# One product of an output stage split once more into seven, with its operand sums on GpSimd

## The chip, the cores and the metric

The kernel runs on one core of a Trainium2 chip. The metric is the device time of one execution in microseconds, the median of several runs.

## The reference

Eight batches of linear attention feed one layer of a feed-forward network. q, k and v are 8 x 8 heads x 576 x 64, all float32.

```python
q_s = softmax(q, over the 64 of a head);  k_s = softmax(k, over the 576 of the sequence)
kv  = einsum('bhsd,bhse->bhde', k_s, v)
x   = einsum('bhsd,bhde->bhse', q_s, kv)        # laid out as 4608 tokens x 512
h   = x @ w_in                                  # 512 x 2048
g   = 0.5 * h * (1 + erf(h / sqrt(2)))          # gelu
out = g @ w_out                                 # 2048 x 512
```

## The kernel before

Everything is worked in bfloat16 with float32 sums in PSUM. The 4608 tokens are worked in nine chunks of 512: chunk c (0 to 7) is the first 512 tokens of batch c, chunk 8 the 64 left over of each batch. The program is written out by hand in the order in which each engine gets its instructions; there is no scheduler, so the order in the code is the order in each engine's queue.

A steady chunk (3 to 7) has an h part and a y part. The h part (`h_waves`) computes h with one level of Strassen-Winograd's scheme (seven products for eight) and the gelus on ScalarE, which write g. The operand sums for the products are made by VectorE: `x_sums` makes t1 to t4 out of xT (the tile quad_t), `s_parts` makes s1 to s4 out of g (tiles s5 and s12; s3 overwrites a quarter of g). The y part (`y_phase`) computes the output in the same scheme. Its seven products have 16 matmuls each (two groups of 128 tokens, eight steps of the contraction, 256 columns). They are issued in the order 1, 5, 6, 2, 7, 3, 4, into the three PSUM banks pa (products 1, 6, 7, 4, accumulated), pb (5, then 3) and pc (2). In the code's names the four quarters of the chunk's output are c11, c12, c21 and c22, in two SBUF tiles y_sb. Between the products VectorE and ScalarE combine the banks into them:

```python
tt(two(pb), two(pa), c22)                # after 6: pb = pa + c22, to which product 3 adds
...
tt(c22, two(pa), c22)                    # after 7
...
mm(3, pb, False)
nc.scalar.copy(out=c12, in_=two(pb))
y_store(c, 0, ysb[0])
after(3)
mm(4, pa, False)
```

`tt` (L430) is the helper behind nearly all of VectorE's tensor operations, so they all have its line. L686 is the matmul of `y_phase`, L739 that of the last chunk (`y_last`, whose last product is made in two halves of 128 columns into banks named yd), L498 that of `h_waves`.

The attention of later batches is spread over the y parts through the table `ins`: after product 5 come the exponentials of k of batch nb = c + 2 and the casts of v on GpSimd (`cast_v_all`, L190), after product 6 the sums of q on VectorE (`q_sums`: one long reduce, L263, and a reciprocal) and the scaling of q on GpSimd (`q_scale_parts`, L278), and the loads of batch nb + 1. After product 3 comes `next_x`: the eight matmuls that make x of chunk c + 1 (L353; in chunk 7, 64 small ones, L358) into four banks, their copies into xT (two on ScalarE, two on VectorE), the DMA transpose of q of batch nb, and, where nb is under 8 (c up to 5), the 72 small matmuls of kv (L225) with their normalization. In chunks 6 and 7 there is no kv, in chunk 7 no `q_sums` either. Product 4 follows on TensorE, then the h part of the next chunk.

`touch_s` is a copy of one element on GpSimd that makes GpSimd wait for VectorE's last operand sum before it goes on, so that its work in the y part runs beside PSUM work of VectorE. The banks of PSUM have roles (bb, ba, x0 to x3, kv0, kv1) which `turn_roles` passes round from chunk to chunk. Chunk 2's h part has an order of its own (`mid` is set there). DMAs are issued on SP's queue, in the last chunk on ScalarE's too.

Of the kernel before, what the change touches and what calls it, by code (L numbers as in the profile page):

```python
# [16 lines left out]
def kernel(  # L17
# [174 lines left out]
    def cast_v_all(b):  # L192
        for hp in range(HP):
            cast_v(b, hp, nc.gpsimd)
# [88 lines left out]
    def norm_q(b, i=0, n=1, eng=None):  # L283

        q_sums(b, i, n)
        q_scale(b, eng or nc.gpsimd, i, n)
# [74 lines left out]
                            start=(bb == 0), stop=True, skip_group_check=True,  # L361
                        )

    def x_all(b, banks):

        if "xT" not in st[b]:
            st[b]["xT"] = attn_sb.tile([128, HP, M], BF16, tag="xT", name="xT", bufs=1)
        for hp, i in enumerate(banks):
            st[b][f"x{hp}"] = bank(i)
        x_mm(b, 0)  # L370
        x_mm(b, 1)
        for hp, eng in ((0, "s"), (1, "v"), (2, "s"), (3, "v")):
            x_evac(b, hp, eng)

    def x_evac(b, hp, eng="v"):
# [19 lines left out]
    def s_parts(c, p0, n, which):  # L395

        g = st[c]["g"]
        a, b = slice(p0, p0 + n), slice(p0 + HK, p0 + HK + n)
        lo, hi = slice(0, HT), slice(HT, M)
        a11, a12, a21, a22 = g[:, a, lo], g[:, b, lo], g[:, a, hi], g[:, b, hi]  # L400
        s1, s2, s4 = s5[:, a], s12[:, a, lo], s12[:, a, hi]
        ops = {
            1: (s1, a21, a22, ALU.add), 2: (s2, s1, a11, ALU.subtract),
            3: (a21, a11, a21, ALU.subtract), 4: (s4, a12, s2, ALU.subtract),
        }
        for i in which:
            tt(*ops[i])
# [21 lines left out]
    def tt(out, in0, in1, op=ALU.add, eng=nc.vector):  # L429
        eng.tensor_tensor(out=out, in0=in0, in1=in1, op=op)  # L430
# [33 lines left out]
    def h_waves(c, mid):  # L464
# [7 lines left out]
        sum_w = {3: 3, 5: 0, 6: 1, 7: 2}  # L472
        lo, hi = slice(0, HT), slice(HT, M)
        bank_of = {
            "A": ("bb", "x0", "x3", "ba"), "B": ("kv0", "kv1", "x1", "x2"), "C": ("x1", "x2", "kv0", "kv1"),
        }
        if mid:
            bank_of.update(B=("kv0", "kv1") * 2, C=("x1", "x2") * 2)
# [127 lines left out]
            mm(4, 2, 3)  # L606
        gelu("B", 2, 3)
        gelu("A", 2, 3)
        s_parts(c, 0, 4, (2, 3, 4) if mid else (3, 4))
        s_parts(c, 4, 4, (1, 2, 3, 4))  # L610
        turn_roles()
        if mid:
            roles.update(ba=roles["x2"], x2=roles["ba"])
# [37 lines left out]
    def y_store(c, half, y_sb):  # L651
        j = 2 * half
        dst = out[c * S:c * S + M, :].rearrange("(p j) n -> p j n", j=J)[:, j:j + 2, :]
        nc.sync.dma_start(out=dst, in_=y_sb)
# [4 lines left out]
    def y_operands(c):  # L659
# [8 lines left out]
        }  # L668
        return act, wgt

    def y_phase(c, ins):

        act, wgt = y_operands(c)
        at = {"ya": 2, "yb": 0, "yc": 3} if c == 1 else {"ya": roles["ba"], "yb": roles["bb"], "yc": roles["x0"]}
        pa, pb, pc = (bank(at[n], n) for n in ("ya", "yb", "yc"))
        ysb = [moe_sb.tile([128, 2, DM], FP32, tag="y_sb", name="y_sb", bufs=2) for i in range(2)]
        c11, c12 = ysb[0][:, :, 0:HN], ysb[0][:, :, HN:DM]
        c21, c22 = ysb[1][:, :, 0:HN], ysb[1][:, :, HN:DM]

        def two(ps):  # L680
            return ps.rearrange("p (j n) -> p j n", j=2)

        def mm(m, ps, first):
            for j in range(2):
                for k in range(HK):
                    nc.tensor.matmul(  # L686
                        ps[:, j * HN:(j + 1) * HN], act[m][:, k, j * 128:(j + 1) * 128],
                        wgt[m][:, k, :], start=(first and k == 0 and j == 0),
                        stop=(k == HK - 1), skip_group_check=True,
                    )  # L690

        def after(i):
            for fn in ins.get(i, []):
                fn()

        mm(1, pa, True)
        (nc.vector.tensor_copy if c == 1 else nc.scalar.copy)(out=c11, in_=two(pa))
        after(1)
        mm(5, pb, True)
        nc.vector.tensor_copy(out=c22, in_=two(pb))  # L700
        after(5)
        mm(6, pa, False)
        tt(two(pb), two(pa), c22)
        after(6)
        mm(2, pc, True)
        tt(c11, c11, two(pc))
        after(2)
        mm(7, pa, False)
        tt(c22, two(pa), c22)
        after(7)  # L710
        mm(3, pb, False)
        nc.scalar.copy(out=c12, in_=two(pb))  # L712
        y_store(c, 0, ysb[0])
        after(3)
        mm(4, pa, False)
        nc.scalar.copy(out=c21, in_=two(pa))
        y_store(c, 1, ysb[1])
        after(4)

    def y_last(c):  # L720

        act, wgt = y_operands(c)
        sets = (("ba", "bb", "x0"), ("x2", "x1", "x3"))
        banks = [[bank(roles[r], n)[:, 0:HN] for r, n in zip(s, ("ya", "yb", "yc"))] for s in sets]
        ysb = [moe_sb.tile([128, 2, DM], FP32, tag="y_sb", name="y_sb", bufs=2) for i in range(2)]
        dst = out.rearrange("(j u s) n -> u s j n", j=J, u=2)

        def store(half, j, c0, engs, us=(0, 1)):
            for u, eng in zip(us, engs):
                eng.dma_start(  # L730
                    out=dst[u, M:S, 2 * half + j, c0:c0 + HN],
                    in_=ysb[half][u * R:(u + 1) * R, j, c0:c0 + HN],
                )

        sp, both = nc.sync, (nc.scalar, nc.sync)

        def mm(j, m, ps, first, n=slice(0, HN)):
            for k in range(HK):
                nc.tensor.matmul(  # L739
                    ps[:, n], act[m][:, k, j * 128:(j + 1) * 128], wgt[m][:, k, n],  # L740
                    start=(first and k == 0), stop=(k == HK - 1), skip_group_check=True,
                )

        for j in range(2):
            mm(j, 1, banks[j][0], True)
            nc.scalar.copy(out=ysb[0][:, j, 0:HN], in_=banks[j][0])
        for j in range(2):
            pa, pb, pc = banks[j]
            c11, c12 = ysb[0][:, j, 0:HN], ysb[0][:, j, HN:DM]
            c21, c22 = ysb[1][:, j, 0:HN], ysb[1][:, j, HN:DM]  # L750
            mm(j, 5, pb, True)
            if j:
                store(0, 0, HN, both, (0,))
                store(1, 0, 0, both, (0,))
            nc.scalar.copy(out=c22, in_=pb)
            mm(j, 6, pa, False)
            tt(pb, pa, c22)
            mm(j, 2, pc, True)
            tt(c11, c11, pc)
            store(0, j, 0, both if j else (sp, sp))  # L760
            mm(j, 7, pa, False)
            tt(c22, pa, c22)
            if j:
                nc.scalar.copy(out=c21, in_=pa)
            store(1, j, HN, both if j else (sp, sp))
            mm(j, 3, pb, False)
            nc.scalar.copy(out=c12, in_=pb)
            if j:
                store(0, j, HN, both)
                for r, n in (("kv0", slice(0, 128)), ("kv1", slice(128, HN))):  # L770
                    ps = bank(roles[r], "yd")
                    mm(j, 4, ps, True, n)
                    tt(c21[:, n], c21[:, n], ps[:, n])
                store(1, j, 0, both)
            else:
                store(0, j, HN, (sp,), (1,))
                mm(j, 4, pa, False)
                nc.scalar.copy(out=c21, in_=pa)
                store(1, j, 0, (sp,), (1,))
# [235 lines left out]
    for m in (3, 2, 4, 1):  # L1015
# [11 lines left out]

    y_phase(1, {
        1: [sums[3], lambda: norm_q(2, 0, 2)],
        6: [lambda: norm_q(2, 1, 2, nc.vector), lambda: cast_v_all(3), lambda: xbar_step(2), lambda: exp_q(3)],  # L1030
        2: [lambda: kv_step(2), lambda: exp_k(3)],
        7: [lambda: q_sums(3)],
        3: [lambda: table(AF.Gelu)],
# [12 lines left out]

        nc.gpsimd.tensor_copy(out=scr[:, 2:3], in_=s12[:, HK - 1, HT:HT + 1])

    def next_x(c, nb):
        x_all(c + 1, [roles[n] for n in ("x0", "x1", "x2", "x3")])  # L1050
        if nb <= B:
            xbar_step(nb)
        if nb < B:
            kv_tiles(nb, (roles["kv0"], roles["kv1"]))
            kv_step(nb, lambda: x_sums(c + 1, (1,)))
            x_sums(c + 1, (2,))
        else:
            x_sums(c + 1, (1, 2))

    for c in range(2, B + 1):  # L1060
        nb = c + 2
        h_waves(c, q_late if c == 2 else None)
        yi = {}
        if nb <= B:
            yi[1] = [lambda: exp_q(nb)]
            yi[6] = [lambda: q_sums(nb), lambda: q_scale_parts(nb)]
            yi[7] = [lambda: table(AF.Gelu)]
        if nb + 1 < B:
            yi[6].append(lambda: load(nb + 1))
        elif nb + 1 == B:  # L1070
            yi[6].append(load_qrest)
        if nb < B:
            yi[5] = [lambda: exp_k(nb), touch_s, lambda: cast_v_all(nb)]
        if c < B:
            yi[3] = [lambda: next_x(c, nb)]
            y_phase(c, yi)
        else:
            y_last(c)
# [30 lines left out]
```

## Time and profile before

| what | value |
|---|---|
| median of 3 runs | 257.45 us (257.31 to 257.54) |
| profiled execution | 257.79 us |
| its span | 255.7 us |
| granted TensorE clock | 0.998 |
| busy: TensorE | 248.6 us, 97% |
| busy: VectorE | 189.8 us, 74% |
| busy: ScalarE | 189.1 us, 74% |
| busy: GpSimd | 53.9 us, 21% |

PE is TensorE, PEld its weight loads, DVE VectorE, ACT ScalarE, POOL GpSimd, SP the queue that issues DMAs. A q behind an engine's name (ACTq) is its sequencer. A group's row gives the line, the engine, the operation with the tiles that it writes and reads, shapes and count, then the busy time, the mean length of one in ns, and the idle time ahead of them. The timeline gives the start, the length and the instructions, with merged equal ones; lengths of merged rows include the overlap of one instruction with the next. Product 1 starts at 85.40 in chunk 2, 111.52 in chunk 3, 137.33 in chunk 4, 163.08 in chunk 5, 188.89 in chunk 6, 214.01 in chunk 7 and 239.23 in chunk 8.

### The profile page before, as it was taken

The numbers are of one execution on the slowest core, as the hardware profiler recorded it, in microseconds if no ns is written. First come the engines' busy times: TensorE is split into PE (matmuls) and PEld (weight loads), VectorE is DVE, ScalarE is ACT, GpSimd is POOL, SyncE is SP. The second block draws the span as 40 slices with busy tenths as digits, with TensorE's granted clock in tenths as the row PEclk, the third lists the DMA queues.
The fourth block names the chain that finished last, engine by engine and source line by source line (L and its number), as shares of the span: only waits on it lengthen the run. The fifth ranks groups of instructions, "written<-read, shape, count | busy, mean of one in ns | idle before, by whom it ended". The sixth has DMA issues, their size and how long they took to land.

```text
span 255.7 us, 6526 instructions
## 1 busy us (share of the span) xinstructions
PE 248.6 (97%) x2678; PEld 195.8 (77%) x2678; DVE 189.8 (74%) x337; ACT 189.1 (74%) x323; POOL 53.9 (21%) x85
## 2 busy tenths in 40 slices
PE   7899999999999999999999999999999999999993
PEld 3444444448888888888888888888888888888883
DVE  1878698877987985898589858985798689448931
ACT  4776878699887986899688968895887687068711
POOL 1530023000705065005500560056000700000000
PEclk9999999999999999999999999999999999999999
DMA  7999999994289997933693369203400240040033
GB/s 239 401 363 424 402 408 398 399 410 178 53 256 380 267 355 234 318 143 102 228 313 142 91 222 245 45 0 118 133 3 0 103 145 3 0 167 3 0 82 86
DMA packets 43166, 50.23 MB, mean 196 GB/s; under 512 B 20224, under 2 KB 30464, under 8 KB 42880
## 3 DMA queue, kind: packets, MB, share of 16 engines
q1 hardware_dynamic: 42416, 49.13, 56.5%
q10 hardware_dynamic: 720, 0.69, 1.1%
q8 instruction: 21, 0.34, 0.5%
q14 instruction: 9, 0.07, 0.1%
HBM read 36.70 MB, written 9.44 MB: 180 GB/s over the span
## 4 chain that ended last, share of the span: by engine, by line
PE 79%; DMA 16%; DVE 1%; issue 1%; ACT 1%; ACTq 0%; SPq 0%
PE ya L686 19%; PE qa L498 19%; PE yb L686 9%; PE qb L498 9%; DMA w<-in_moe_w_in_dram 6%; PE ps L387 6%; DMA f<-in_k_dram 5%; PE qc L498 5%; PE yc L686 5%; DMA f<-in_v_dram 3%; PE ya L739 2%; DMA touch<-in_moe_w_in_dram 2%; PE yb L739 1%; PE kv L225 1%; PE ps L353 1%; DVE s L430 1%
## 5 line engine op out<-in xcount | busy, mean ns | idle before, releaser
L498 PEld LDWEIGHTS <-quad_s 128*128 128x128 bf16 x448 | 43.8, 98 | 5.2
L686 PEld LDWEIGHTS <-g 128*128 128x128 bf16 x448 | 43.2, 98 | 6.0 <-issue 0.4
L686 PEld LDWEIGHTS <-s 128*128 128x128 bf16 x336 | 32.8, 98 | 4.2 <-DVE s L430 0.4
L498 PEld LDWEIGHTS <-wi_bf 128*128 128x128 bf16 x336 | 32.9, 98 | 4.0 <-issue 0.2
L278 POOL TENSOR_TENSOR e<-e,recq 128x256 bf16<-128x256 bf16 x40 | 24.2, 642 | 30.7 <-DVE recq L264 21.1
L498 PE MATMUL qa<-quad_t,quad_s 128*128 128x256 bf16 x224 | 29.2, 273 | 0.0
L430 DVE TENSOR_TENSOR qb<-qa,r 128x512 f32<-128x512 f32 x28 | 18.2, 695 | 14.2 <-PE qa L498 9.6
L387 PE MATMUL ps<-xT,wi_bf 128*128 128x512 bf16 x128 | 28.1, 379 | 0.2 <-ACT xT L380 0.2
L686 PE MATMUL yb<-wo_bf,s 128*128 128x256 bf16 x224 | 26.9, 273 | 0.1
L686 PE MATMUL ya<-w,g 128*128 128x256 bf16 x224 | 26.8, 273 | 0.0
L263 DVE TENSOR_REDUCE qsum<-e 128x16 f32<-128x1024 bf16 (+1 forms) x12 | 20.9, 1740 | 4.6 <-ACT e L173 4.5
L387 PEld LDWEIGHTS <-wi_bf 128*128 128x128 bf16 x128 | 12.4, 98 | 15.3 <-issue 0.7
L393 ACT ACTIVATE g<-ps 128x512 bf16<-128x512 f32 x32 | 17.6, 602 | 6.2 <-PE ps L387 5.8
L173 ACT ACTIVATE e<-f 128x512 bf16<-128x512 f32 (+1 forms) x42 | 20.5, 557 | 2.0 <-DMA f<-in_q_dram 1.9
L522 ACT ACTIVATE g<-r 128x512 bf16<-128x512 f32 x28 | 17.3, 631 | 6.1 <-DVE r L430 6.1
L522 ACT ACTIVATE g<-qc 128x512 bf16<-128x512 f32 x28 | 15.2, 594 | 7.5 <-PE qc L498 7.5
L269 POOL TENSOR_TENSOR e<-e,recq 128x1024 bf16<-128x1024 bf16 (+1 forms) x4 | 9.3, 2330 | 48.5 <-DVE recq L264 41.9
L430 DVE TENSOR_TENSOR r<-qa,r 128x512 f32<-128x512 f32 x28 | 18.0, 683 | 0.9 <-PE qa L498 0.7
L178 ACT ACTIVATE ek<-f 128x2304 bf16<-128x2304 f32 (+1 forms) x10 | 17.2, 1726 | 1.1 <-DMA f<-in_k_dram 1.1
L190 POOL CAST v_aug<-f 128x576 bf16<-128x576 f32 x25 | 17.0, 716 | 3.6 <-DMA f<-in_v_dram 3.5
L378 DVE CAST xT<-ps 128x512 bf16<-128x512 f32 x18 | 11.6, 682 | 8.0 <-PE ps L353 6.4
L712 ACT COPY y_sb<-yb 128x512 f32<-128x512 f32 x7 | 4.1, 585 | 17.2 <-PE yb L686 16.1
(96 smaller groups left out, 442.0 us busy)
## 6 DMA issues: line engine op xcount, KB each, us to landing
out_dram<-y_sb SPq DMA_DIRECT2D x16, 512.0 KB, 3.4
f<-in_k_dram SPq DMA_DIRECT2D x6, 1152.0 KB, 9.6
f<-in_v_dram SPq DMA_DIRECT2D x6, 1152.0 KB, 9.2
f<-in_q_dram SPq DMA_DIRECT2D x6, 1024.0 KB, 7.0
w<-in_moe_w_in_dram SPq DMA_DIRECT2D x6, 512.0 KB, 9.0
f<-in_v_dram SPq DMA_DIRECT2D x8, 288.0 KB, 6.5
f<-in_q_dram SPq DMA_DIRECT2D x4, 512.0 KB, 8.9
w<-in_moe_w_out_dram SPq DMA_DIRECT2D x2, 1024.0 KB, 11.5
```

The source lines that it names most:

```text
L173: nc.scalar.activation(out=dst[:, i], in_=src[:, u], func=AF.Exp)
L178: nc.scalar.activation(out=ek[b % 2][:, i:i + n], in_=st[b]["kf"][:, i:i + n].rearrange("p x (n d) -> p x n d", n=NS), func=AF.Exp,)
L190: eng.tensor_copy(out=o, in_=i)
L263: nc.vector.reduce_sum(out=qsum, in_=st[b]["eq"][:, :, i * w:(i + 1) * w, :], axis=AX.X)
L278: nc.gpsimd.tensor_tensor(out=e, in0=e, op=ALU.mult, in1=st[b]["recq"][:, j, i:i + 4].unsqueeze(2).to_broadcast([128, 4, D]),)
L378: nc.vector.tensor_copy(out=st[b]["xT"][:, hp, :], in_=ps)
L387: nc.tensor.matmul(ps, wi_bf[:, dm, t * 128:(t + 1) * 128], st[c]["xT"][:, dm, :], start=(dm == 0), stop=(dm == NDM - 1),)
L393: nc.scalar.activation(out=st[c]["g"][:, t, :], in_=ps, func=AF.Gelu)
L430: eng.tensor_tensor(out=out, in0=in0, in1=in1, op=op)
L498: nc.tensor.matmul(held[kind, q][:, u], w, mov[m][:, k], start=(m in (1, 5) and u == 0 and k == 0), stop=(k == 1), skip_group_check=True,)
L522: nc.scalar.activation(out=g[:, t:t + 2, half], in_=held[kind, q], func=AF.Gelu)
L686: nc.tensor.matmul(ps[:, j * HN:(j + 1) * HN], act[m][:, k, j * 128:(j + 1) * 128], wgt[m][:, k, :], start=(first and k == 0 and j == 0), ...
```

## The change

In chunks 3 to 7 product 3 (s4 of g by the lower right quarter of w_out) is no longer 16 matmuls of 256 columns into pb but seven second-level products ("sets"), each of four matmuls of 128 columns, 28 in all, each with a weight load of its own as before. Sets 1, 6 and 7 go into a quarter of the bank kv1 (the tile yd, `D`), sets 2, 3, 4 and 5 into the four quarters of the bank of pb (the tile yf, `X`). Set 1 stands behind product 6, sets 6, 5, 2, 4, 3 and 7 behind product 7, where product 3 was. The sums of operands that the sets need are made by GpSimd: four sums of weights once, in chunk 1's y part (`two_begin`, which takes over the buffer of an earlier v), and four sums of s4 in each of the chunks (`sums`, behind `touch_s` after product 5). They are 128 x 512 each.

On VectorE pb = pa + c22 becomes c12 = pa + c22 in SBUF, and five adds bring the sets into c12: a (set 1's u to a quarter), b (u with set 6, to a quarter), c (u with set 7, to two quarters), then, inside `next_x`, e (all of X) and d (one quarter of X again). The add c22 = pa + c22 after product 7 is queued behind c.

Further: one xT copy of `next_x` goes from VectorE to ScalarE in these chunks, and ScalarE's c12 copy falls away; the store of c12 is issued behind `next_x`, so behind the transpose on SP; the first two banks of `h_waves` change places; the casts of v are queued ahead of the h part in chunks 3 to 5; in chunk 2 the sum s1 of rows 4 to 7 is made ahead of s4 of rows 0 to 3; in the last chunk VectorE copies c12 of the second half instead of ScalarE.

```diff
-    def x_all(b, banks):
+    def x_all(b, banks, engs="svsv"):
...
-        for hp, eng in ((0, "s"), (1, "v"), (2, "s"), (3, "v")):
+        for hp, eng in enumerate(engs):
             x_evac(b, hp, eng)
...
-            "A": ("bb", "x0", "x3", "ba"), "B": ("kv0", "kv1", "x1", "x2"), "C": ("x1", "x2", "kv0", "kv1"),
+            "A": ("x0", "bb", "x3", "ba"), "B": ("kv0", "kv1", "x1", "x2"), "C": ("x1", "x2", "kv0", "kv1"),
...
-        s_parts(c, 0, 4, (2, 3, 4) if mid else (3, 4))
-        s_parts(c, 4, 4, (1, 2, 3, 4))
+        if mid:
+            s_parts(c, 0, 4, (2, 3))
+            s_parts(c, 4, 4, (1,))
+            s_parts(c, 0, 4, (4,))
+            s_parts(c, 4, 4, (2, 3, 4))
+        else:
+            s_parts(c, 0, 4, (3, 4))
+            s_parts(c, 4, 4, (1, 2, 3, 4))
...
+    class Two:
...
+        def halves(self, t, ks):
+            return [[t[:, b + 2 * ks.start:2 * ks.stop:2, n:n + 128] for n in (0, 128)] for b in range(2)]
+
+        def weights(self):
+            (b11, b12), (b21, b22) = self.halves(self.raw_w(), slice(0, 4))
+            t1, t2, t3, t4 = (self.w[:, i] for i in range(4))
+            for o, i0, i1 in ((t1, b12, b11), (t2, b22, t1), (t3, b22, b12), (t4, b21, t2)):
+                tt(o, i0, i1, ALU.subtract, eng=nc.gpsimd)
...
+        def sums(self, c):
+
+            (a11, a21), (a12, a22) = self.halves(y_operands(c)[0][self.m], slice(0, 4))
+            s1, s2, s3, s4 = (self.s[:, i] for i in range(4))
+            tt(s1, a21, a22, eng=nc.gpsimd)
+            for o, i0, i1 in ((s2, s1, a11), (s4, a12, s2), (s3, a11, a21)):
+                tt(o, i0, i1, ALU.subtract, eng=nc.gpsimd)
...
+        def mm(self, *sets):
+
+            lo, hi = slice(0, 128), slice(128, 256)
+            A, W, w, s = self.A, self.W, self.w, self.s
+            for m in sets:
+                for i in range(4):
+                    e, o = 2 * i, 2 * i + 1
+                    lhs, rhs, at, r = {
+                        1: (A[:, e, lo], W[:, e, lo], "D", 0),
+                        2: (A[:, o, lo], W[:, o, lo], "X", 0),
+                        3: (s[:, 3, i], W[:, o, hi], "X", 1),
+                        4: (A[:, o, hi], w[:, 3, i], "X", 2),
+                        5: (s[:, 0, i], w[:, 0, i], "X", 3),
+                        6: (s[:, 1, i], w[:, 1, i], "D", 0),
+                        7: (s[:, 2, i], w[:, 2, i], "D", 0),
+                    }[m]
+                    first = at not in self.begun
+                    self.begun.add(at)
+                    nc.tensor.matmul(
+                        getattr(self, at)[:, r * 128:(r + 1) * 128], lhs, rhs,
+                        start=first, stop=(i == 3), skip_group_check=True,
+                    )
+
+        def add(self, what, out):
...
+            X = self.X.rearrange("p (j n m) -> p j n m", j=2, n=2)
+            u = self.D[:, 0:128]
+            o = out.rearrange("p j (n m) -> p j n m", n=2)
+            for i in what:
+                t, x = {
+                    "a": (o[:, 0, 0], u), "b": (o[:, 0, 1], u),
+                    "c": (o[:, 1], u.unsqueeze(1).to_broadcast([128, 2, 128])),
+                    "d": (o[:, 0, 1], X[:, 1, 1]), "e": (o, X),
+                }[i]
+                tt(t, t, x)
...
         mm(6, pa, False)
-        tt(two(pb), two(pa), c22)
+        if t3:
+            tt(c12, halves(pa), c22)
+            t3.begin(c, bank(at["yb"], "yf"), bank(roles["kv1"], "yd"))
+            t3.mm(1)
+            t3.add("a", c12)
+        else:
+            tt(halves(pb), halves(pa), c22)
         after(6)
         mm(2, pc, True)
...
         mm(7, pa, False)
-        tt(c22, two(pa), c22)
+        if t3:
+            t3.mm(6, 5, 2, 4, 3)
+            t3.add("b", c12)
+            t3.mm(7)
+            t3.add("c", c12)
+        tt(c22, halves(pa), c22)
         after(7)
-        mm(3, pb, False)
-        nc.scalar.copy(out=c12, in_=two(pb))
-        y_store(c, 0, ysb[0])
-        after(3)
+        if not t3:
+            mm(3, pb, False)
+            nc.scalar.copy(out=c12, in_=halves(pb))
+            y_store(c, 0, ysb[0])
+            after(3)
+        else:
+            ins[3][0](lambda: t3.add("ed", c12))
+            y_store(c, 0, ysb[0])
         mm(4, pa, False)
...
             mm(j, 3, pb, False)
-            nc.scalar.copy(out=c12, in_=pb)
+            (nc.vector.tensor_copy if j else nc.scalar.copy)(out=c12, in_=pb)
...
-    def next_x(c, nb):
-        x_all(c + 1, [roles[n] for n in ("x0", "x1", "x2", "x3")])
+    def next_x(c, nb, fn=lambda: None):
+        x_all(c + 1, [roles[n] for n in ("x0", "x1", "x2", "x3")], "svsv" if c == 2 else "svss")
         if nb <= B:
             xbar_step(nb)
+
+        def first():
+            x_sums(c + 1, (1,))
+            fn()
+
         if nb < B:
             kv_tiles(nb, (roles["kv0"], roles["kv1"]))
-            kv_step(nb, lambda: x_sums(c + 1, (1,)))
-            x_sums(c + 1, (2,))
-        else:
-            x_sums(c + 1, (1, 2))
+            kv_step(nb, first)
+        else:
+            first()
+        x_sums(c + 1, (2,))
...
     for c in range(2, B + 1):
         nb = c + 2
+        if 2 < c < B - 2:
+            cast_v_all(nb)
...
         if nb < B:
-            yi[5] = [lambda: exp_k(nb), touch_s, lambda: cast_v_all(nb)]
+            yi[5] = [lambda: exp_k(nb), touch_s]
+            if c == 2:
+                yi[5].append(lambda: cast_v_all(nb))
+        if 2 < c < B:
+            yi.setdefault(5, []).append(lambda: two[3].sums(c))
```

More of the change, by code (lines that the diff above doesn't have):

```diff
@@ L669, in y_operands, with __init__, raw_w, begin @@
         return act, wgt
+    class Two:
+        def __init__(self, m, w, s):
+            self.m, self.w, self.s = m, w, s
+        def halves(self, t, ks):
[5 more added lines that the diff above has]
+                tt(o, i0, i1, ALU.subtract, eng=nc.gpsimd)
+        def raw_w(self):
+            return wo_bf[:, DN, HN:DM]
+        def sums(self, c):
[4 more added lines that the diff above has]
+                tt(o, i0, i1, ALU.subtract, eng=nc.gpsimd)
+        def begin(self, c, X, D):
+            self.A, self.W = y_operands(c)[0][self.m], self.raw_w()
+            self.X, self.D = X, D
+            self.begun = set()
+        def mm(self, *sets):
[30 more added lines that the diff above has]
+                tt(t, t, x)
@@ L671, in y_phase, with two_begin @@
+    def two_begin():
+        t = f32in.tile([128, 9, 512], BF16, tag="vf1", name="two", bufs=1)
+        two[3] = Two(3, *(t[:, i:i + 4].rearrange("p x (i n) -> p x i n", i=4) for i in (0, 4)))
+        two[3].weights()
+    two = {}
     def y_phase(c, ins):
@@ L678, in y_phase, with halves @@
         c21, c22 = ysb[1][:, :, 0:HN], ysb[1][:, :, HN:DM]
-        def two(ps):
+        def halves(ps):
             return ps.rearrange("p (j n) -> p j n", j=2)
@@ L694, in after @@
                 fn()
+        t3 = two[3] if c > 2 else None
         mm(1, pa, True)
-        (nc.vector.tensor_copy if c == 1 else nc.scalar.copy)(out=c11, in_=two(pa))
+        (nc.vector.tensor_copy if c == 1 else nc.scalar.copy)(out=c11, in_=halves(pa))
         after(1)
         mm(5, pb, True)
-        nc.vector.tensor_copy(out=c22, in_=two(pb))
+        nc.vector.tensor_copy(out=c22, in_=halves(pb))
         after(5)
         mm(6, pa, False)
-        tt(two(pb), two(pa), c22)
+        if t3:
[5 more added lines that the diff above has]
+            tt(halves(pb), halves(pa), c22)
         after(6)
         mm(2, pc, True)
-        tt(c11, c11, two(pc))
+        tt(c11, c11, halves(pc))
         after(2)
         mm(7, pa, False)
-        tt(c22, two(pa), c22)
-        after(7)
-        mm(3, pb, False)
-        nc.scalar.copy(out=c12, in_=two(pb))
-        y_store(c, 0, ysb[0])
-        after(3)
+        if t3:
[4 more added lines that the diff above has]
+        tt(c22, halves(pa), c22)
+        after(7)
+        if not t3:
[6 more added lines that the diff above has]
+            y_store(c, 0, ysb[0])
         mm(4, pa, False)
-        nc.scalar.copy(out=c21, in_=two(pa))
+        nc.scalar.copy(out=c21, in_=halves(pa))
         y_store(c, 1, ysb[1])
@@ L1029 @@
         1: [sums[3], lambda: norm_q(2, 0, 2)],
-        6: [lambda: norm_q(2, 1, 2, nc.vector), lambda: cast_v_all(3), lambda: xbar_step(2), lambda: exp_q(3)],
+        6: [lambda: norm_q(2, 1, 2, nc.vector), lambda: cast_v_all(3), two_begin, lambda: xbar_step(2), lambda: exp_q(3)],
         2: [lambda: kv_step(2), lambda: exp_k(3)],
@@ L1072 @@
         if nb < B:
-            yi[5] = [lambda: exp_k(nb), touch_s, lambda: cast_v_all(nb)]
+            yi[5] = [lambda: exp_k(nb), touch_s]
[3 more added lines that the diff above has]
+            yi.setdefault(5, []).append(lambda: two[3].sums(c))
         if c < B:
-            yi[3] = [lambda: next_x(c, nb)]
+            yi[3] = [lambda *fn: next_x(c, nb, *fn)]
             y_phase(c, yi)
```

## The prediction

> **What bounds the kernel now.** I read the page's busy shares first, then the chain of waits, then TensorE and VectorE beside each other in the timeline of one steady chunk, and last the groups by form for prices.
>
> ```profile
> PE 248.6 (97%) x2678; PEld 195.8 (77%) x2678; DVE 189.8 (74%) x337; ACT 189.1 (74%) x323; POOL 53.9 (21%) x85
> PE 79%; DMA 16%; DVE 1%; issue 1%; ACT 1%; ACTq 0%; SPq 0%
> ```
>
> TensorE is the bound: busy 97% of the span, and apart from the loads at the start the chain that ends last is TensorE nearly throughout. A matmul taken away is worth its time, and a wait put into TensorE's queue costs its whole length. The chain shows TensorE waiting for VectorE in chunk 2, and in chunk 6 product 3, the next x and product 4 back to back:
>
> ```profile
> 86.55 1.29 DVE s L430 x2
> 87.84 0.05 issue
> 87.89 1.48 PE yb L686 x12
> ...
> 197.79 1.75 PE yb L686 x16
> 199.54 0.56 PE ps L353 x8
> 200.09 1.85 PE ya L686 x16
> ```
>
> In chunk 2, product 5 stops after four of its 16 matmuls until the sum s1 of rows 4 to 7 is written. The timeline of chunk 4, TensorE and then VectorE, from the end of product 3 on (product 1 starts at 137.33):
>
> ```profile
> 147.90 0.63 PE L353 MATMUL ps<-qT,kvc 64*64 64x512 bf16 x8
> 148.36 0.81 PE L225 MATMUL kv<-v_aug,ek 64*64 64x65 bf16 x72
> 149.10 1.92 PE L686 MATMUL ya<-w,g 128*128 128x256 bf16 x16
> ...
> 143.44 2.28 DVE L263 TENSOR_REDUCE qsum<-e 128x32 f32<-128x2048 bf16 x1
> 145.75 0.35 DVE L264 RECIPROCAL recq<-qsum 128x32 f32<-128x32 f32 x1
> 146.02 0.63 DVE L430 TENSOR_TENSOR y_sb<-y_sb,yc 128x512 f32<-128x512 f32 x1
> 146.56 0.68 DVE L430 TENSOR_TENSOR y_sb<-ya,y_sb 128x512 f32<-128x512 f32 x1
> 148.39 1.29 DVE L378 CAST xT<-ps 128x512 bf16<-128x512 f32 x2 [1.15 <-PE ps L353]
> ```
>
> Product 4 accumulates into the bank that the c22 add (146.56) reads. That add ends at 147.24, 1.86 us before product 4 starts at 149.10; VectorE then idles 1.15 us. This slack is what the change spends.
>
> **The change, part by part.** All times below count from the start of product 1 of a chunk.
>
> *Fewer matmul columns.* The prices:
>
> ```profile
> L686 PE MATMUL yb<-wo_bf,s 128*128 128x256 bf16 x224 | 26.9, 273 | 0.1
> L739 PE MATMUL yd<-w,g 128*128 128x128 bf16 x16 | 1.1, 219 | 0.0
> L430 DVE TENSOR_TENSOR y_sb<-ya,y_sb 128x256 f32<-128x256 f32 x2 | 0.8, 424 | 0.9 <-PE ya L739 0.9
> L430 DVE TENSOR_TENSOR y_sb<-y_sb,yd 128x128 f32<-128x128 f32 x2 | 0.6, 286 | 1.1 <-PE yd L739 1.0
> ```
>
> Means are latencies of overlapping matmuls, so I take spacings. Products of 16 start 1.747 us apart (139.08 to 140.82 and so on), 109.2 ns a matmul. The 16 matmuls of yd are the very form that the change uses, one weight load each: 1.06 us from first start to last end, less the last one's 219 ns, over 15 gaps is 56 ns. Product 3 goes from 16 x 109.2 = 1.747 to 28 x 56 = 1.563 us: -0.185 us a chunk, -0.92 over chunks 3 to 7.
>
> The Trainium skill speaks against this step: "TensorE: Matmul & The Clock Gate", section "Back-to-back issue gap", gives about 81 ns for a 128-column matmul in a stream of weight loads and matmuls, and calls the 56 ns an isolated figure. By that, an estimate from the page, product 3 would take 2.27 us and lose 0.52 a chunk; the yd row is such a stream and shows 56, and the measurement decides here.
>
> *The second-level adds on VectorE.* One 512-wide add into PSUM becomes one into SBUF (0.70, same), and adds a (0.29), b (0.29), c (0.42), e (0.65) and d (0.29) come in; ScalarE loses the c12 copy and takes one of VectorE's two xT copies (0.6 each). Where they stand in the queue decides. Set 1 stands behind product 6, so sets 6, 5, 2, 4, 3 start at 5 x 1.747 + 0.22 = 8.96, and set 7, which writes the bank that b reads, at 8.96 + 20 x 0.0558 = 10.08.
>
> - b: VectorE's reduce starts after add a, about 6.4; reduce, reciprocal and the c11 add (2.28, 0.35, 0.63, starts overlapping by 0.09) bring b to 9.6 to 9.9. Set 7 goes at 10.08: 0.15 to spare.
> - c: set 7's last matmul ends at 10.46. Handing on takes 0.055 each way (yd's last end 251.64 to the add's start 251.70; in chunk 2 s1's end 87.83 to product 5 at 87.89). c runs 10.52 to 10.94.
> - kv: half its matmuls write the bank that c reads. Before they start at 148.36 - 137.33 = 11.03, now 0.185 earlier, 10.85, and must wait to 10.99. Bounds: 0.08 to 0.17 for c between 0.36 and 0.45; I take 0.135. That leaves -0.05 in each of chunks 3 to 5: **-0.15**.
> - c22 is now queued behind c: 10.85 to 11.53, and product 4 may start at 11.59. In chunks 3 to 5 TensorE arrives at 11.77 - 0.05 = 11.72, so kv covers it by 0.13. In chunk 6 there is no kv: product 4 began at 200.03 - 188.89 = 11.14, now 11.59: **+0.45** net of the saving. In chunk 7 the 64 small matmuls of x take its place, 225.25 - 214.01 = 11.24: **+0.35**. Bounds for each are 0.1 around these (0.1 is the spread of the adds' rows and handoffs).
> - Next chunk: the bank of e and d is free by 13.6, and its first matmul, in a swapped order, comes at 13.9. The sum t2 ends at about 14.7, wanted at 15.2; beside GpSimd the same sum took 0.60 for 0.41 (150.73 against 149.60), so 0.2 or 0.4 of that 0.5 may go. Cost nothing; if gone, the excess.
>
> *GpSimd's sums.* No row has 512 columns on GpSimd in bf16; 256 take 0.61 (L278) and 1024 take 1.90 (L269). On the line between, 1.04; ends 0.61 and 1.90. They start behind the touch, which ran at 141.09 = 3.76, so four end at about 8.1, and the last is wanted at 10.08. recq comes at about 9.1 (8.77 before), so q's scaling is hardly later. The v casts go ahead of the h part; GpSimd is idle there, and v's next load starts earlier for it. The four weight sums fall into the 8.4 us that GpSimd waits in chunk 1 and 2 (its wait on ScalarE's r in the list of waits). SP's transpose now stands ahead of the c12 store, 26 us before that buffer is wanted. All nothing.
>
> *Chunk 2's order.* s1 of rows 4 to 7 moves ahead of s4: it starts at 86.55 for 87.15 (ScalarE's last gelu for it ends at 86.34), so product 5's fifth matmul needn't wait from 87.58 to 87.89: **-0.31**.
>
> *The end.* c12 of the last half is copied by VectorE, idle 0.96 us there, not by ScalarE:
>
> ```profile
> 251.31 0.68 DVE L430 TENSOR_TENSOR y_sb<-y_sb,yd 128x128 f32<-128x128 f32 x2 [0.96 <-PE yd L739]
> 251.41 0.37 ACT L767 COPY y_sb<-yb 128x256 f32<-128x256 f32 x1 [0.66 <-PE yd L739]
> 251.81 1.41 ACTq L730 DMA_DIRECT2D out_dram<-y_sb  x2
> ```
>
> ScalarE's copy stood behind a DMA issue until 251.41, so c12's stores went at 251.81 and the last two at 252.37 and 252.40. The copy would now end near 251.22, c12's stores go at 251.41, the last at 252.02, when yd's second add is done. Gain 0.35 if an issue takes 0.5 as at 251.81, none if 1.0 as the one before it; I take **-0.25**.
>
> Sum: -0.15 + 0.45 + 0.35 - 0.31 - 0.25 = +0.09. The profiled execution took 257.79 (255.7 span and 2.1 around it), so 257.88; it ran 0.34 above the median of the runs, to which the change applies alike: 257.45 + 0.09 = 257.5.
>
> **The rivals.** A measurement of this kernel can tell about 0.2%, 0.51 us, from no change.
>
> *Faster: the waits for c and c22 hardly bite.* All of the columns' saving then stays: -0.92 - 0.31 - 0.25 = -1.48, 255.97; with half of the waits (0.4 of kv, 0.64 and 0.53 of product 4, 1.57 together) it is -0.69, 256.8. For it: VectorE's work on PSUM could take less than the rows; against: all links of the chain are rows. From a c22 done at 11.3 it decides. 0.21.
>
> *Slower: VectorE is the bound from b on.* The margin at b is 0.15 and at product 4 in chunks 3 to 5 it is 0.13. If the reduce or the adds run 0.3 later than the rows, set 7, c, c22 and product 4 all slip: 0.15 in each of chunks 3 to 6 at b, with 0.05 or more a chunk for t2 and the bank behind it, +0.8, 258.3. For it: two dependent adds stand ahead of the reduce, each unable to overlap; against: those 0.09 gaps are counted. 0.19.
>
> *The 128-column matmuls are spaced 81 ns, not 56.* With weights from three tiles in turn this is 28 x 25 = 0.70 more a chunk, with c and c22 later by the same: +3.5, 261.0. 0.03.
>
> *GpSimd is late.* Decides from 1.5 us a sum. At 1.90 the last ends at 11.6, set 7 waits 1.5, five times: 265. The stretch is clear of VectorE's bf16 sums. 0.04.
>
> **How the numbers follow.** The forecast has 0.53, with its own range 257.1 to 257.9 from the bounds (0.1 on five waits, 0 to 0.35 at the end), which is nearly all inside 0.51. Faster by over 0.2%: the first rival and a small part of the forecast, 0.24. Slower: the last three, 0.26, of which the forecast's upper edge adds little. Within: 0.50. The range takes in the halved waits and VectorE's lateness, and leaves the full saving, 81 ns and GpSimd outside: 256.4 to 258.6.
>
> **What would show it.** Right: small matmuls 56 ns apart; product 4 at 11.6 in chunks 6 and 7, with TensorE waiting there for VectorE's c22 add; kv stopping about 0.13 in chunks 3 to 5; no stop of product 5 in chunk 2; the last stores issued at about 252.0 less the shift; chunks 3 to 5 about 0.05 shorter. Wrong: a wait on GpSimd at sets 5, 6, 3 or 7, a stop ahead of set 7, chunks 6 and 7 not longer, or the first matmuls of the next chunk waiting for e, d or t2.

## The result: 0.3% slower

The changed kernel takes 258.29 us (median of 8 runs, 257.93 to 258.45), the kernel before beside it 257.43 (257.31 to 257.75): a ratio of 1.0029, 95% interval 1.0018 to 1.0040, so 0.46 to 1.03 us more. The profiled executions differ by as much: spans of 256.54 and 255.69.

The pitch from one product 1 to the next, in the two traces, says where (chunk 8: from its product 1 to the end of the span; all in us):

| chunk | 2 | 3 | 4 | 5 | 6 | 7 | 8 |
|---|---|---|---|---|---|---|---|
| before | 26.13 | 25.81 | 25.75 | 25.81 | 25.12 | 25.23 | 16.45 |
| after | 25.81 | 26.13 | 26.13 | 25.81 | 25.80 | 25.54 | 16.03 |
| difference | -0.32 | +0.32 | +0.37 | 0.00 | +0.69 | +0.32 | -0.42 |

The ends of the row are near the forecast (-0.31 and -0.25). The surprise is the middle: chunks 3 to 5 were forecast 0.05 shorter each, and chunk 6 came out 0.24 longer than its forecast of +0.45. The page's shares (busy time, then the chain by engine) say what kind of loss it is: TensorE has less to do than before (247.9 for 248.6), and VectorE now has 6% of the chain for 1%. That share is the length of the VectorE operations that TensorE had to follow, not the length of TensorE's stops, which are counted below.

```profile
PE 247.9 (97%) x2738; PEld 195.7 (76%) x2738; DVE 198.7 (77%) x358; ACT 189.5 (74%) x322; POOL 82.1 (32%) x109
PE 87%; DVE 6%; DMA 4%; issue 1%; ACT 0%; ACTq 0%; POOL 0%; DVEq 0%
```

Chunk 4 of the changed kernel in the timeline, the same stretch that was shown of before; product 1 starts at 137.23. TensorE, then VectorE, then GpSimd:

```profile
146.19 0.39 PE L726 MATMUL yd<-two 128*128 128x128 bf16 x4
146.41 0.39 PE L726 MATMUL yf<-two 128*128 128x128 bf16 x4
...
147.31 0.39 PE L726 MATMUL yd<-two 128*128 128x128 bf16 x4
147.62 0.63 PE L353 MATMUL ps<-qT,kvc 64*64 64x512 bf16 x8
148.08 0.89 PE L225 MATMUL kv<-v_aug,ek 64*64 64x65 bf16 x72
148.90 1.92 PE L768 MATMUL ya<-w,g 128*128 128x256 bf16 x16
150.66 1.19 PE L498 MATMUL qa<-xT,wi_bf 128*128 128x256 bf16 x8
151.68 1.04 PE L498 MATMUL qb<-quad_t,quad_s 128*128 128x256 bf16 x8
152.87 0.83 PE L498 MATMUL qa<-quad_t,quad_s 128*128 128x256 bf16 x6
...
146.86 0.28 DVE L430 TENSOR_TENSOR y_sb<-y_sb,yd 128x128 f32<-128x128 f32 x1
147.73 0.42 DVE L430 TENSOR_TENSOR y_sb<-y_sb,yd 128x256 f32<-128x256 f32 x1 [0.60 <-PE yd L726]
148.07 0.68 DVE L430 TENSOR_TENSOR y_sb<-ya,y_sb 128x512 f32<-128x512 f32 x1
148.67 0.68 DVE L378 CAST xT<-ps 128x512 bf16<-128x512 f32 x1
149.45 0.82 DVE L430 TENSOR_TENSOR quad_t<-xT 128x512 bf16<-128x512 bf16 x1
150.20 0.99 DVE L430 TENSOR_TENSOR y_sb<-y_sb,yf 128x512 f32<-128x512 f32 x2
...
151.92 0.89 DVE L430 TENSOR_TENSOR quad_t<-xT,quad_t 128x512 bf16<-128x512 bf16 x1
...
146.53 4.79 POOL L278 TENSOR_TENSOR e<-e,recq 128x256 bf16<-128x256 bf16 x8 [0.64 <-issue]
151.27 2.88 POOL L190 CAST v_aug<-f 128x576 bf16<-128x576 f32 x4
```

A merged row of eight matmuls without a stop is 1.04 long. The qa row at 150.66 has 1.19: TensorE stopped for 0.16 in it. The qa row at 152.87 starts 1.19 after the qb row instead of 0.87: 0.32 lost. The first stop is for the bank that adds e and d (the row at 150.20) read, the second for t2 (151.92). Both come from VectorE's queue, and in it two sums of xT are longer than before: t1 (149.45) takes 0.82 for 0.41, t2 0.89 for 0.60. GpSimd works beside both. But GpSimd worked beside both in the kernel before, too:

```profile
149.60 0.41 DVE L430 TENSOR_TENSOR quad_t<-xT 128x512 bf16<-128x512 bf16 x1
150.73 0.60 DVE L430 TENSOR_TENSOR quad_t<-xT,quad_t 128x512 bf16<-128x512 bf16 x1
146.24 4.82 POOL L278 TENSOR_TENSOR e<-e,recq 128x256 bf16<-128x256 bf16 x8 [2.52 <-ACT ek L178]
```

What differs is how much of a GpSimd operation is left when the sum starts. These are the single operations under way at the four starts, two of the kernel before, then two of the changed one:

```profile
149.09 0.61 POOL L278 TENSOR_TENSOR e<-e,recq 128x256 bf16<-128x256 bf16 x1
150.44 0.61 POOL L278 TENSOR_TENSOR e<-e,recq 128x256 bf16<-128x256 bf16 x1
...
149.38 0.61 POOL L278 TENSOR_TENSOR e<-e,recq 128x256 bf16<-128x256 bf16 x1
151.87 0.67 POOL L190 CAST v_aug<-f 128x576 bf16<-128x576 f32 x1
```

Before, 0.10 is left for t1 and 0.32 for t2; in the changed kernel 0.54 and 0.62. Each sum takes that rest and 0.28 more, or 0.41 if the rest is short. The nine traces of this case have 216 sums of xT behind product 1 of chunk 2. In the 76 that start with more than 0.13 of a GpSimd operation to go, the length less that rest is 0.27 to 0.28; the other 140 take 0.41 to 0.43. So these sums behave as if they waited out the GpSimd operation under way; what VectorE does inside that time isn't shown.

Chunk 7 has no GpSimd work there, and t1 is short:

```profile
227.19 0.43 DVE L430 TENSOR_TENSOR quad_t<-xT 128x512 bf16<-128x512 bf16 x1
```

In chunks 6 and 7 product 4 waits for the c22 add as forecast (the timeline names the releaser):

```profile
200.74 1.91 PE L768 MATMUL ya<-w,g 128*128 128x256 bf16 x16 [0.55 <-DVE y_sb L430]
226.54 1.91 PE L768 MATMUL ya<-w,g 128*128 128x256 bf16 x16 [0.45 <-DVE y_sb L430]
```

From the spacing of single matmuls, start to start, come TensorE's stops that the kernel before doesn't have: kv 0.11 in each of chunks 3 to 5; product 4 0.62 in chunk 6 and 0.52 in chunk 7; the bank of e and d 0.11, 0.16, 0.16 and 0.27 behind chunks 3 to 6; t2 0.32 and 0.31 behind chunks 3 and 4. Together 2.79, against 0.92 of saved columns, 0.31 in chunk 2 and 0.42 at the end. That leaves 1.14, where the pitches sum to 0.96 more than before; 0.06 of the difference is a stop of the kernel before in the h part of chunk 6, which the changed one doesn't have, and the rest isn't traced.

### The profile page after: what moved, and what is told of

The parts are those of the page before. It is cut to its first block, busy times and chain, and to the rows that moved or that the text cites. A ratio compares the mean times of both kernels' runs of the same rounds, so it can differ in the third digit from the quotient of the medians.

```text
span 256.5 us, 6691 instructions
## 1 busy us (share of the span) xinstructions
PE 247.9 (97%) x2738; PEld 195.7 (76%) x2738; DVE 198.7 (77%) x358; ACT 189.5 (74%) x322; POOL 82.1 (32%) x109
## 4 chain that ended last, share of the span: by engine, by line
PE 87%; DVE 6%; DMA 4%; issue 1%; ACT 0%; ACTq 0%; POOL 0%; DVEq 0%
PE qa L498 19%; PE ya L768 17%; PE ps L387 11%; PE qb L498 9%; PE yb L768 6%; PE ps L641 5%; PE qc L498 5%; PE yc L768 5%; DVE y_sb L430 3%; PE ya L837 2%; DMA f<-in_v_dram 2%; DMA touch<-in_moe_w_in_dram 2%; PE yf L726 2%; DVE quad_t L430 2%; PE yb L837 1%; PE yd L726 1%
## 5 line engine op out<-in xcount | busy, mean ns | idle before, releaser
L768 PEld LDWEIGHTS <-s 128*128 128x128 bf16 x256 | 25.0, 98 | 2.9
L380 ACT CAST xT<-ps 128x512 bf16<-128x512 f32 x23 | 12.3, 593 | 16.7 <-PE ps L358 8.4
L387 PEld LDWEIGHTS <-wi_bf 128*128 128x128 bf16 x128 | 12.4, 98 | 15.2 <-issue 0.5
L430 POOL TENSOR_TENSOR two<-s 128x512 bf16<-128x512 bf16 x10 | 11.6, 1157 | 31.1 <-DVE s L430 31.1
L190 POOL CAST v_aug<-f 128x576 bf16<-128x576 f32 x25 | 18.0, 756 | 4.1 <-DMA f<-in_v_dram 3.1
L768 PE MATMUL yb<-wo_bf,s 128*128 128x256 bf16 x144 | 17.2, 273 | 0.0
```

The lines of the kernel that those rows point to most:

```text
L190: eng.tensor_copy(out=o, in_=i)
L387: nc.tensor.matmul(ps, wi_bf[:, dm, t * 128:(t + 1) * 128], st[c]["xT"][:, dm, :], start=(dm == 0), stop=(dm == NDM - 1),)
L768: nc.tensor.matmul(ps[:, j * HN:(j + 1) * HN], act[m][:, k, j * 128:(j + 1) * 128], wgt[m][:, k, :], start=(first and k == 0 and j == 0), ...
```

## The experiments

Each pair of numbers below is a median of the kernel and a ratio to the kernel before on the same chip, with its 95% interval. For c22 ahead of c, the run without casts, chunks 3 to 5 alone and the two small edits that kernel before took 257.77, beside the changed kernel 257.43; a difference of medians to the changed kernel is uncertain by that 0.34 there. The traces give these differences from product 1 of chunk 2 to the end: 2.15 less than the changed kernel with c22 ahead of c, 0.68 without the casts, 1.00 with chunks 3 to 5 alone, 1.33 without the scaling.

**c22 ahead of c.** TensorE's set 7 is under way while VectorE idles 0.60 ahead of c; c22, which needs product 7 alone, is put there.

```diff
             t3.add("b", c12)
+            tt(c22, halves(pa), c22)
             t3.mm(7)
             t3.add("c", c12)
-        tt(c22, halves(pa), c22)
+        else:
+            tt(c22, halves(pa), c22)
```

> The add c22 = pa + c22 is queued ahead of add c instead of behind it, in chunks 3 to 7; nothing else changes. Theory (VectorE's queue behind set 7 is too long, and 0.60 us ahead of c it stands idle): c22 goes into that idle stretch, product 4 waits no more in chunks 6 and 7 (0.62 and 0.52 us), and all that VectorE does behind c comes 0.6 earlier, so that the waits of the next chunk for the bank of e and d (0.11, 0.16, 0.16 in chunks 3 to 5; 0.27 in chunk 6 stays at about 0.25, since TensorE comes earlier too) and for t2 (0.32 twice) go: 2.2 us less than the changed kernel, about 256.1. Rival (GpSimd's hold on the shared reads decides when t1 and t2 get done, not VectorE's queue): the bank and t2 waits stay, only 1.1 us less, about 257.2.

Measured: 256.22, ratio 0.9942 (0.9930 to 0.9955). That is 2.1 less than the changed kernel, and 1.5 less than the kernel before. Chunk 4 of it, VectorE:

```profile
146.49 0.28 DVE L430 TENSOR_TENSOR y_sb<-y_sb,yd 128x128 f32<-128x128 f32 x1
146.68 0.68 DVE L430 TENSOR_TENSOR y_sb<-ya,y_sb 128x512 f32<-128x512 f32 x1
147.36 0.42 DVE L430 TENSOR_TENSOR y_sb<-y_sb,yd 128x256 f32<-128x256 f32 x1
147.74 0.69 DVE L378 CAST xT<-ps 128x512 bf16<-128x512 f32 x1
148.53 0.80 DVE L430 TENSOR_TENSOR quad_t<-xT 128x512 bf16<-128x512 bf16 x1
...
150.98 0.86 DVE L430 TENSOR_TENSOR quad_t<-xT,quad_t 128x512 bf16<-128x512 bf16 x1
```

c22 fits between b and c. t1 and t2 are still as long (0.80, 0.86), but they come early enough: the stops for the bank in chunks 3 to 5, for t2 and for c22 are gone from the spacing, and only kv's 0.11 and one of 0.31 for the bank in chunk 6 are left. The first theory holds; the rival, by which GpSimd alone would set when t1 and t2 are done, falls. GpSimd's part is a length, VectorE's queue is what turned it into a wait.

**Without the casts of chunks 3 to 5.**

```diff
-        if 2 < c < B - 2:
-            cast_v_all(nb)
```

> The changed kernel without GpSimd's casts of v of batches 5 to 7 (the kernel leaves them out and works with older v there). Theory (t2 is slow since a cast of GpSimd beside it holds it up, 0.89 instead of 0.41 us): t2 takes 0.41 to 0.43 in chunks 4 and 5, TensorE's wait for it (0.32 twice) falls to nothing, 0.6 us less than the changed kernel, 257.7. Rival (t2 is late only because adds e and d are queued ahead of it): t2 starts as late as now, and the waits shrink by less than 0.1 each, 258.1.

Measured: 257.58, ratio 0.9997 (0.9988 to 1.0006), 0.7 less than the changed kernel. In chunk 4, t1 and t2 on VectorE:

```profile
149.21 0.83 DVE L430 TENSOR_TENSOR quad_t<-xT 128x512 bf16<-128x512 bf16 x1
...
151.68 0.41 DVE L430 TENSOR_TENSOR quad_t<-xT,quad_t 128x512 bf16<-128x512 bf16 x1
```

The kernel leaves the casts out and works with older v. In its trace t2 is short without casts beside it, t1, which runs beside the scaling of q, is not. The stops for t2 are gone, those for the bank (0.16) stay. So the casts cost 0.3 in each of chunks 3 and 4 (25.81 for 26.13), in the changed kernel.

**The casts moved, in the kernel before.** The same move of the casts, put into the kernel before and nothing else.

```diff
+        if 2 < c < B - 2:
+            cast_v_all(nb)
...
-            yi[5] = [lambda: exp_k(nb), touch_s, lambda: cast_v_all(nb)]
+            yi[5] = [lambda: exp_k(nb), touch_s]
+            if c == 2:
+                yi[5].append(lambda: cast_v_all(nb))
```

> The kernel before, with the casts of v ahead of the h part in chunks 3 to 5 as in the change, and nothing else. Theory (beside the casts t2 and t3 get slower, but there VectorE has some 0.7 us to spare before TensorE wants t2): t2 or t3 takes 0.8 to 0.9 us in chunks 4 and 5, TensorE doesn't wait, the same time as before within 0.1, 257.4 to 257.8. Rival (the casts cost by themselves what was seen, 0.32 in each of two chunks): 0.6 more than before, 258.2.

Measured: 257.49, ratio 1.0001 (0.9993 to 1.0010): no change. t2 and t3 in chunk 4, beside GpSimd:

```profile
150.44 0.60 DVE L430 TENSOR_TENSOR quad_t<-xT,quad_t 128x512 bf16<-128x512 bf16 x1
150.97 0.88 DVE L430 TENSOR_TENSOR quad_t<-xT 128x512 bf16<-128x512 bf16 x1
...
150.71 2.27 POOL L190 CAST v_aug<-f 128x576 bf16<-128x576 f32 x3
```

t3 (0.88) is held up as t2 was in the change (0.89), and nobody waits. t2 takes 0.60 although the casts follow the scaling without a gap: it starts when 0.32 of a scaling is left. The move costs nothing by itself; in the changed kernel the casts cost 0.6, on top of a queue that had no slack left.

**Without GpSimd's scaling in chunks 3 to 6.**

```diff
-            yi[6] = [lambda: q_sums(nb), lambda: q_scale_parts(nb)]
+            yi[6] = [lambda: q_sums(nb)] + ([lambda: q_scale_parts(nb)] if c == 2 else [])
```

> The changed kernel without GpSimd's scaling of q in the y parts of chunks 3 to 6 (left out: q of those batches stays unscaled). Theory (t1 takes 0.82 instead of 0.42 us since a scaling of GpSimd runs beside it, and that lateness goes on through e and d to their bank): t1 takes 0.42, the waits for the bank (0.11, 0.16, 0.16, 0.27) go to nothing; the casts that now come earlier are done before t2, so t2 takes 0.42 and its two waits of 0.32 go as well; the waits for c22 in chunks 6 and 7 stay (0.62, 0.52). Together 1.3 less than the changed kernel, 257.0. Rival (the adds e and d in the queue are the whole cause): t1 shorter, but the waits stay above half, 0.5 less or under, 257.8.

Measured: 256.85, ratio 0.9974 (0.9964 to 0.9984), 1.4 less than the changed kernel. Chunk 4:

```profile
148.73 0.43 DVE L430 TENSOR_TENSOR quad_t<-xT 128x512 bf16<-128x512 bf16 x1
149.07 1.00 DVE L430 TENSOR_TENSOR y_sb<-y_sb,yf 128x512 f32<-128x512 f32 x2
...
150.80 0.41 DVE L430 TENSOR_TENSOR quad_t<-xT,quad_t 128x512 bf16<-128x512 bf16 x1
```

The kernel leaves the scaling out, and the casts, now earlier, are over before t1 starts (by 147.61). Both sums are short, no stop for the bank or for t2 is left, and the stops for c22 in chunks 6 and 7 are unchanged (0.62, 0.52). So two things had to meet for the stops at the bank and at t2 of chunks 3 to 5: sums made longer by GpSimd, and a queue in which c22 stood late; taking away either one is enough. e and d take 1.00 here and 0.99 beside GpSimd: the adds that read PSUM aren't held up, the sums of xT with both operands in SBUF are.

The Trainium skill has this rule in "SBUF — State Buffer", section "Who interferes with whom": a VectorE instruction with two SBUF inputs contends with a GpSimd instruction that reads SBUF, because its second input comes through a read interface that the two share, and one with at most one SBUF input, outside the modes that use two ports, does not. The rows above agree (0.43 to 0.82 for t1, 1.00 and 0.99 for e and d).

**The seven products in chunks 3 to 5 alone.**

```diff
-        t3 = two[3] if c > 2 else None
+        t3 = two[3] if 2 < c < 6 else None
...
-        if 2 < c < B:
+        if 2 < c < 6:
             yi.setdefault(5, []).append(lambda: two[3].sums(c))
```

(The xT copies of `next_x` go with it.)

> The changed kernel with the seven small products in chunks 3 to 5 alone; chunks 6 and 7 make product 3 as before. Theory (chunks 6 and 7 lose by c22, having no kv to cover it): chunk 6 gets shorter by 0.62 + 0.27 - 0.19 = 0.70 and chunk 7 by 0.52 - 0.19 = 0.33, together 1.0 less than the changed kernel, 257.3. Rival (the loss sits in the next chunk's start in general): 0.3 less, 258.0.

Measured: 257.26, ratio 0.9983 (0.9974 to 0.9992), 1.0 less than the changed kernel. Chunks 6 and 7 are back at 25.12 and 25.23, product 4 of chunk 6 starts at once:

```profile
200.24 1.92 PE L768 MATMUL ya<-w,g 128*128 128x256 bf16 x16
202.00 1.04 PE L498 MATMUL qa<-xT,wi_bf 128*128 128x256 bf16 x8
```

Chunks 3 and 4 keep their 26.14. So about 1.0 of the loss belongs to chunks 6 and 7, the two without kv, with the 0.27 for the bank behind chunk 6 in it. Chunks 3 and 4, which keep their loss, have the other 0.7.

**Two of the small edits alone**, in the kernel before: s1 of rows 4 to 7 first in chunk 2, and VectorE for the last c12.

```diff
+        if mid:
+            s_parts(c, 0, 4, (2, 3))
+            s_parts(c, 4, 4, (1,))
+            s_parts(c, 0, 4, (4,))
+            s_parts(c, 4, 4, (2, 3, 4))
...
-            nc.scalar.copy(out=c12, in_=pb)
+            (nc.vector.tensor_copy if j else nc.scalar.copy)(out=c12, in_=pb)
```

> The kernel before with two of the small edits alone: s1 of rows 4 to 7 ahead of s4 in chunk 2, and VectorE copying the last c12. Theory: they are worth what they were in the changed kernel's trace, 0.31 and 0.25 to 0.42, so 0.56 to 0.73 less than before, 256.8. Rival (the end's gain is only variation of the DMA issues): 0.3 less, 257.1.

Measured: 256.69, ratio 0.9966 (0.9954 to 0.9978), 0.57 to 1.19 less than before. Its trace has chunk 2 at 25.81 (0.32 less) and chunk 8 at 16.21 (0.24 less), 0.56 together, at the lower edge of what was measured. Another 0.34 of the difference in its profiled execution lies ahead of chunk 2's product 1 (85.06 for 85.40), where nothing was changed; the other kernels have that start between 85.0 and 85.4 too.

**e and d ahead of t1 as well**, on top of c22 ahead of c, for the 0.31 that was left in chunk 6.

```diff
         def first():
-            x_sums(c + 1, (1,))
             fn()
+            x_sums(c + 1, (1,))
```

> The kernel with c22 ahead of c, in which also adds e and d go ahead of t1, in chunks 3 to 7. Theory (the bank of e and d is what TensorE waits for in chunk 6, and t1 isn't wanted until 0.87 us after the h part starts): the 0.31 in chunk 6 goes, nothing comes in its place; 0.3 less than with c22 ahead of c alone (256.2), 255.9. Rival (t1, now behind e and d, gets too late for product 5 of the h part): a wait of 0.1 to 0.3 there in each chunk, 256.4 to 257.2.

Measured: 255.63, ratio 0.9934 (0.9921 to 0.9946), 1.4 to 2.0 less than the kernel before. Chunk 6, TensorE and VectorE:

```profile
199.14 1.92 PE L768 MATMUL ya<-w,g 128*128 128x256 bf16 x16
200.90 1.04 PE L498 MATMUL qa<-xT,wi_bf 128*128 128x256 bf16 x8
201.77 1.04 PE L498 MATMUL qb<-quad_t,quad_s 128*128 128x256 bf16 x8
...
199.68 1.00 DVE L430 TENSOR_TENSOR y_sb<-y_sb,yf 128x512 f32<-128x512 f32 x2
200.59 0.65 DVE L430 TENSOR_TENSOR quad_t<-xT 128x512 bf16<-128x512 bf16 x1
```

qa, qb follow without a stop. That the 0.31 went is shown by the trace; the interval overlaps that of c22 ahead of c alone. Chunks 3 to 7 have pitches of 25.70, 25.65, 25.65, 24.93 and 25.04, shorter than the kernel before by 0.10 to 0.18; what is left there is kv's 0.11 in chunks 3 to 5. This version beats both kernels, with every part of the change kept, and c22 and the pair of e and d moved in VectorE's queue. In its trace 0.74 of the gain lies in chunks 3 to 7, where the seven products are, and as much again (0.32 and 0.42) in chunk 2 and at the end, where the two small edits work.

The xT copy on ScalarE, the swapped banks and the later store of c12 weren't run alone; no stop is put down to them.

## Why the prediction was right or wrong, point by point

The range held the time, since the rivals had widened it: the forecast's own 257.1 to 257.9 didn't hold it. A time within 0.2% of before had the largest chance, and it came out slower by 0.3%, +0.86 against a forecast sum of +0.09. One of the prediction's own signs of being wrong appeared: the first matmuls of the next chunk waited for e, d and t2. By its steps:

- **Columns: right.** A set of four small matmuls takes 0.22 (146.19 to 146.41 and so on in chunk 4), 56 ns a matmul, weight load by weight load; the rival at 81 ns falls.
- **kv: right**, 0.11 for 0.135.
- **c22: right in place and size.** Stops of 0.62 and 0.52, expected 0.64 and 0.53. The run with chunks 3 to 5 alone and the one with c22 ahead of c both take them out. What the prediction didn't see is that the stop was avoidable: it took the place of c22 behind c as given, while its own figures have VectorE idle between b, done at 9.9, and c, from 10.52.
- **Next chunk, "Cost nothing": this is the step that failed.** The prediction gave d 13.6 and the bank 13.9, and let the sums beside GpSimd lose 0.2 or 0.4, in t2 alone. It took t1's 0.41 of before (149.60) for the length of a sum without GpSimd beside it, but a scaling ran there too, with 0.10 left at t1's start. In the changed kernel t1, which stands ahead of e and d, starts when 0.54 of a scaling is left and takes 0.82, so d ended at 13.96 in chunk 4 (151.19 - 137.23) and TensorE stopped 0.16. And t2 took 0.89, not the 0.60 that it had beside GpSimd before, since 0.62 of a cast was left at its start instead of 0.32 of a scaling. It ended at 15.58 (152.81 - 137.23), not 14.7, and was wanted at 15.2. The two made 0.69 for the bank and 0.63 for t2, 1.32 in all for a term set at nothing. The run without casts takes out the stops for t2 alone; the one without scaling, where the casts come early as well, takes out both.
- **Chunk 2: right**, 0.32 for 0.31. **The end: right in place**, somewhat larger: the span's end came 0.42 nearer to product 1 of chunk 8, forecast 0.25; the last stores went 0.34 earlier by that count (253.31 - 240.51 against 252.37 - 239.23).
- **GpSimd's sums: right that nothing waits**, small in size: 1.16 each, not 1.04 (144.73 + 1.16 - 137.23 = 8.66 for the last end, wanted at 10.08).
- **The slower rival** named VectorE's lateness, but at b, with the reduce as its cause. b was on time in chunk 4 (146.86 - 137.23 = 9.63), and no chunk has a stop ahead of set 7. VectorE was late further down the queue. The rival's 258.3 lies on the measured 258.29, but that is luck, since 0.6 of its 0.8 was to come from b.

With the failed term at its measured 1.32 the sum would have been +1.41, 0.55 above the measured 0.86. The other terms that came out better (the end by 0.17, the kv stops by 0.08) and the start ahead of chunk 2 (0.10 earlier in the changed kernel's trace, where nothing was changed) account for 0.35 of that; 0.2 stays open, but for the 0.06 of the stop that only the kernel before has in the h part of chunk 6.

## What to carry to other kernels

When work is added to an engine that had slack, lay out its whole queue up to the next point where the bound engine waits for it, with the length that each operation has beside its neighbours of that moment. A length read from one trace holds for the moment at which the operation started there: t1 ran beside GpSimd in both kernels, and took 0.41 in one and 0.82 in the other. A saving of 0.18 us a chunk was lost to a sum that grew by 0.4. Ask of each new wait whether the awaited operation can go into an idle stretch ahead of it: moving c22 by one place was worth 2.1 us, more than the whole saving of columns. And an edit that costs nothing where it is tried alone (the casts) isn't free once its cover is spent elsewhere.

## What the runs showed of the hardware that was not expected

- A VectorE sum of two bf16 SBUF operands (128 x 512) takes 0.41 to 0.43 alone. Beside GpSimd's scalings and casts its length depends on what is left of the GpSimd operation under way at its start: that rest and 0.28 more, 0.48 to 0.90 in these traces, and the usual 0.41 where 0.13 or less is left, even if GpSimd goes on without a gap. f32 adds with one PSUM operand take the same in both cases (0.68 for 128 x 512).
- GpSimd's bf16 sum of 128 x 512 takes 1.16, above the 1.04 on the line between the 0.61 of 256 and the 1.90 of 1024 columns; those two rows are multiplications by a broadcast operand.
